# Attention block and two gated MLPs on one core: piece stores to GpSimd's queue, sum stores to SyncE's, another order on ScalarE

## The chip, the cores and the metric

One core of one Trainium2 chip runs the whole program. The metric is the device time of one execution in microseconds (us). Engines are called PE (TensorE), VectorE (DVE), ScalarE (ACT), GpSimd (POOL) and SyncE (SP); the last one computes nothing and only issues transfers.

## The reference

```python
B, H, S, Ns, D = 8, 8, 512, 32, 64          # x: B,H,S,D   state: B,H,Ns,D

# attention between tokens and a small state, both ways
a     = softmax(scale * x @ state.T)         # tokens look at the state
xread = a @ state
a2    = softmax(scale * state @ x.T)         # the state looks at tokens
sread = a2 @ x
x = concat([xread, sread], axis=2) -> (B * 544, 512)

h = x @ w_in;  x = (h * sigmoid(1.702 * h)) @ w_out      # first MLP, 512 -> 2048 -> 512
h = x @ w_in2; x = (h * cos(h)) @ w_out2                 # second MLP
```

All of it is to be computed to float32 accuracy. The weights come as 64-bit floats.

## The kernel before

**Numbers as two halves.** Every float32 factor of a large product is held as a rounded high half and the rest as a low half (`split_g`, `split_state`), and a product is three matmuls: high by high, high by low, low by high. ScalarE rounds the high half, VectorE subtracts for the low half.

**Tiles and steps.** The 4096 token rows are eight tiles of 512, one for each batch entry; the 256 state rows form a ninth, the tail tile (t = 8). A tile has 16 steps, one for each 128 columns of the hidden layer (c = 0 to 15). The first MLP (m = 0) goes through tiles 0 to 6, the tail tile, then tile 7; the second MLP (m = 1) follows. In each step `hidden` (line 341) makes one 128-wide slice of the hidden layer in PSUM, and `second` (line 422) adds the slice of two steps before (`LAG` = 2) into four PSUM accumulators. In between ScalarE and VectorE apply the gate: `gate` (line 371 on) in the first MLP, `cosine` (line 390) in the second. The order of instructions on each engine is the order in which the program is written, and each engine's queue is first in, first out.

**Decoding weights.** A 64-bit weight is turned into a float32 on the chip, in units of 128 x 1024. `decode_begin` (line 107) gives two ScalarE conversions (lines 117 and 122) and two VectorE bit operations (lines 125 and 128, called `bits`, at the end of the step). `decode_end` (line 134), one step later, rounds the high half on ScalarE (line 141) and subtracts for the low half on VectorE (line 143). Tile 0 decodes a unit in each of steps 0 to 13; the second MLP's weights are decoded in the tail tile, in tile 7 and in the first tile of the second MLP, one unit every second or third step.

**Pieces of state times weight.** For tiles 1 to 7 the state is multiplied into the first weight matrix beforehand, so that a slice of the hidden layer needs six matmuls and not 24 (line 353 in place of line 360). `sw_piece` (line 162) makes one of 64 pieces: six half-wide matmuls into a PSUM bank of the pool `psa` (two banks, shared with the attention's products), the rounding on ScalarE (line 174), the subtraction on VectorE (line 175), and one store to DRAM for each of two tiles (line 178). Its staging tile is two deep (tag `g`). `load_sw` (line 182) fetches the pieces back. The list `sw_steps` (line 503) says at which steps pieces are made; the attention for the next tile (`parts`, line 487) is spread over the same steps and takes banks of the same pool in turn.

**Sums.** At the end of a tile, `store` (line 441) copies each of the four accumulators to SBUF (`o`, two buffers) and stores it to DRAM (`yd`). This happens at step 1 of the next tile, and the accumulators are needed again at step 2. In the first MLP the store was issued on ScalarE's queue (line 446), in the second on SyncE's (line 449).

**Queues.** SyncE issues nearly everything in program order: weights (`fetch_w`), the attention's inputs (`load_xT`, `load_xN`), the pieces' stores and loads. GpSimd does little; among it are the four low halves of the tail tile's input (`split_tail`, line 456, subtraction at line 463), at step 14 of tile 6.

Of the kernel before, what the change touches and what calls it, by code (L numbers as in the profile page):

```python
# [24 lines left out]
KF = DFF // P  # L25
# [16 lines left out]
def attention_two_mlps(  # L42
# [12 lines left out]
    nc = tc.nc  # L55
# [78 lines left out]
    def decode_end():  # L134

        if not begun:
            return lambda: None
        m, nm, j = begun.pop(0)
        u = wt[m, nm, j]
        w = wp.tile([P, 2, UNIT], F32R, name=f"w{nm}{m}_{j}", tag=f"w{nm}{j}")  # L140
        nc.scalar.activation(out=w[:, 0, :], in_=u, func=AF.Copy)
        wt[m, nm, j] = (w[:, 0, :], w[:, 1, :])
        return lambda: nc.vector.tensor_tensor(out=w[:, 1, :], in0=u, in1=w[:, 0, :].bitcast(F32), op=ALU.subtract)
# [18 lines left out]
    def sw_piece(p, f, k):  # L162

        ps = ps_a.tile([P, S], F32, name="psS", tag="psa")
        for e in range(2):
            wh, wl = wt[0, "i", 2 * f + e]
            sl = slice(k * 2 * P, (k + 1) * 2 * P)
            out_ = ps[:, e * 2 * P:(e + 1) * 2 * P]
            for i, (l, r) in enumerate(((rhi, wh), (rhi, wl), (rlo, wh))):
                nc.tensor.matmul(out_, l[:, k, :], r[:, sl], start=(e == 0 and i == 0), stop=(e == 1 and i == 2),  # L170
                                 skip_group_check=True)
        o = ep.tile([P, 4, 2, P], F32R, name="swo", tag="g")
        pv = ps.rearrange("p (c f) -> p c f", f=P)
        nc.scalar.activation(out=o[:, :, 0, :], in_=pv, func=AF.Copy)
        nc.vector.tensor_tensor(out=o[:, :, 1, :], in0=pv, in1=o[:, :, 0, :].bitcast(F32), op=ALU.subtract)  # L175
        r0 = (k % 2) * D
        for i, b in enumerate(PAIRS[p]):
            nc.sync.dma_start(
                out=sw_dram[b, f][r0:r0 + D, :, k // 2, :], in_=o[i * D:(i + 1) * D].bitcast(F32).rearrange("p c h f -> p c (h f)")
            )  # L180

# [189 lines left out]
    def gate(t, c, stores, unit):  # L371

        ph = ht.pop((0, t, c))
        t1 = ep.tile([P, sizes[t]], F32, name="t1", tag="t1")
        nc.scalar.activation(out=t1, in_=ph, func=AF.Tanh, scale=0.5 * GATE)  # L375
        low_w = decode_end()
        g = t1
        nc.vector.scalar_tensor_tensor(out=g, in0=t1, scalar=1.0, in1=ph, op0=ALU.add, op1=ALU.mult)  # L378
        for s in stores[:1]:
            s()  # L380
        low = split_g(0, t, c, g)
        low_w()
        act, bits = decode_begin(*unit) if unit else ((lambda: None),) * 2
        act()
        low()
        for s in stores[1:]:
            s()
        return bits

    def cosine(t, c, stores, before, unit, end):  # L390

        ph = ht[1, t, c]
        r = ep.tile([P, sizes[t]], F32, name="r", tag="t1")
        d = ep.tile([P, sizes[t]], F32, name="d", tag="g")
        nc.scalar.activation(out=r, in_=ph, func=AF.Copy, scale=1.0 / (2.0 * math.pi), bias=0.25)  # L395
        low_w = decode_end()
        low = times(*before) if before else None
        if end:
            low()
        nc.vector.tensor_scalar(out=r, in0=r, scalar1=MAGIC, scalar2=MAGIC, op0=ALU.add, op1=ALU.subtract)  # L400
        for s in stores[:-1]:
            s()
        act, bits = decode_begin(*unit) if unit else ((lambda: None),) * 2
        nc.vector.scalar_tensor_tensor(out=d, in0=r, scalar=-TWO_PI_HI, in1=ph, op0=ALU.mult, op1=ALU.add)
        nc.vector.scalar_tensor_tensor(out=r, in0=r, scalar=-TWO_PI_LO, in1=d, op0=ALU.mult, op1=ALU.add)
        nc.vector.tensor_scalar(out=r, in0=r, scalar1=R_MIN, scalar2=R_MAX, op0=ALU.max, op1=ALU.min)  # L406
        nc.scalar.activation(out=r, in_=r, func=AF.Sin, bias=half_pi)  # L407
        act()
        if low and not end:
            low()  # L410
        low_w()
        for s in stores[-1:]:
            s()
        ht[1, t, c] = (ph, r)
        return bits

    def times(t, c):
        ph, r = ht.pop((1, t, c))
        nc.vector.tensor_tensor(out=r, in0=r, in1=ph, op=ALU.mult)  # L419
        return split_g(1, t, c, r)  # L420
# [20 lines left out]
    def store(m, t, k):  # L441
        n = sizes[t]
        o = op.tile([P, n if m == 0 else DM], F32, name="o", tag="o")
        nc.scalar.activation(out=o, in_=yt[k], func=AF.Copy, scale=0.5 if m == 0 else 1.0)  # L444
        if m == 0:
            nc.scalar.dma_start(out=y_dram[t][:, k, :], in_=o)
        elif t < B:
            r0 = t * TOK + k * P
            nc.sync.dma_start(out=out[r0:r0 + P, :], in_=o)
        else:  # L450
            per = P // NS
            for i in range(per):
                r0 = (k * per + i) * TOK + S
                nc.sync.dma_start(out=out[r0:r0 + NS, :], in_=o[i * NS:(i + 1) * NS, :])
# [23 lines left out]
    def warm(n):  # L478
# [22 lines left out]
    todo = {}  # L501

    sw_steps = (
        ((0, 1), [(0, c) for c in (2, 3, 4, 5, 7, 9, 11, 13, 15)] + [(1, c) for c in range(1, 8)]),
        ((1, 8), [(1, c) for c in (9, 11, 12, 13, 14, 15)] + [(2, c) for c in (0, 2, 3, 4, 5, 6, 8, 9, 10, 11)]),
        ((3, 1), [(t, c) for t in (3, 4) for c in (3, 4, 5, 9, 10, 11, 13, 14)]),
        ((5, 1), [(t, c) for t in (5, 6) for c in (3, 4, 5, 9, 10, 11, 13, 14)]),
    )
    todo_sw = {step: (p, n // 4, n % 4) for p, (_, at_) in enumerate(sw_steps) for n, step in enumerate(at_)}
    todo_split = {step: p for p, (step, _) in enumerate(sw_steps)}  # L510
    scores_of = [1, 0, *range(2, B)]

# [26 lines left out]
    with tc.manual_schedule():  # L539
# [34 lines left out]
        low_w = decode_end()  # L574
# [18 lines left out]
        fetches.update({steps[steps.index((0, B - 1, 0)) + 2 * j + 3]: (1, "o", j) for j in range(KF // 2)})  # L593
        at2 = [(0, B, c) for c in (8, 11, 14)] + [(0, B - 1, c) for c in range(1, KF, 2)] + [(1, 0, c) for c in range(0, 10, 2)]
        units.update({at_: (1, nm, j) for at_, (nm, j) in zip(at2, ((nm, j) for nm in "io" for j in range(KF // 2)))})
        loads_next = {9: (0,), 10: (1,), 11: (2,), 12: (3, 4), 13: (5,), 14: (6,), 15: (7,)}
        for i, (m, t, c) in enumerate(steps):
            if m == 0 and c == 0 and t + 1 < B:
                new_x(("a", t + 1), S, range(2))
                plan(i, t)  # L600
            if i + 1 < len(steps):
                hidden(m, t, c)
            if i + 2 == len(steps):
                hidden(*steps[-1])
            stores = second(*steps[i - LAG]) if i >= LAG else []
            unit = units.get((m, t, c))
            if m == 0:
                bits = gate(t, c, stores, unit)
            else:
                bits = cosine(t, c, stores, steps[i - 1][1:] if steps[i - 1][0] == 1 else None, unit, i + 1 == len(steps))  # L610
            if (m, t, c) in fetches:
                fetch_w(*fetches[m, t, c])
            if m == 0 and (t, c) in todo_split:
                split_state()
            if m == 0 and (t, c - 3) in todo_split and todo_split[t, c - 3] + 1 < len(PAIRS):
                load_pair(todo_split[t, c - 3] + 1)
            for b, name in todo.pop(i, ()):
                run_piece(b, int(name[-1]), name[:-2])
            if m == 0 and (t, c) in todo_sw:
                sw_piece(*todo_sw[t, c])  # L620
            bits()
            if m == 0:
                if t == 0 and c in (7, 9, 11, 13):
                    load_sw(1, (c - 7) // 2)
                if t == 0 and c == KF - 1:
                    for j in range(4, 8):
                        load_sw(1, j)
                if t == 1 and 5 <= c < 13:
                    load_sw(t, c + 3)
                if 1 < t < B and c + 8 < KF:  # L630
                    load_sw(t, c + 8)
                if 0 < t < B - 1:
                    for j in loads_next.get(c, ()) if t == 1 else (c - 8,):
                        if j >= 0:
                            load_sw(t + 1, j)
            if m == 0 and t == B - 2 and c == KF - 2:
                split_tail()
            j = i // KF
            if j + 1 < len(order) and i + KF >= len(steps1):
                if c == 2:  # L640
                    load_y(order[j + 1])
                if c in (7, 9, 11, 13):
                    split_y(order[j + 1], (c - 7) // 2, nc.gpsimd if m else nc.vector)
# [47 lines left out]
```

## Time and profile before

| | |
|---|---|
| median of 3 executions | 1566.74 us (1563.5 to 1567.01) |
| the profiled execution | 1568.79 us, its span 1567.0 us |
| PE busy | 1481.3 us, 95% of the span |
| VectorE, ScalarE, GpSimd busy | 962.5, 646.5, 44.0 us |
| mean granted TensorE clock | 0.978 |
| moved by DMA | 140.58 MB, mean 90 GB/s |

The page shows busy time in slices of the span, the longest chain of work, and groups of instructions by line. Matmuls overlap one another, so a busy PE is not a PE at its peak; but a stretch in which PE is idle or its clock is below 1.00 is time lost when PE sets the pace. The first MLP with the attention takes the first 810 us or so, the second MLP the rest.

### The profile page before, as it was taken

What the parts mean: (1) busy time and instruction counts of PE and PEld (TensorE: products, weight loads), DVE (VectorE), ACT (ScalarE), POOL (GpSimd) and SP (SyncE); (2) the same over time, 40 slices, a digit from 0 to 9 for tenths busy, and PEclk for the clock granted to TensorE, in tenths of its full rate; (3) what the DMA queues carried; (4) which work ended last, traced back from release to release, by engine and by line L of the source; (5) the groups of instructions that cost most, each with busy time, mean ns of one, the idle gap of its engine ahead of it and who ended that gap; (6) DMA issues with size and microseconds to landing.
All of it is one profiled execution on the core that took longest, in us unless ns stands there. A gap on an engine that the chain in (4) does not pass through costs nothing.

```text
span 1567.0 us, 19260 instructions
## 1 busy us (share of the span) xinstructions
PE 1481.3 (95%) x7306; PEld 1204.5 (77%) x7306; DVE 962.5 (61%) x1674; ACT 646.5 (41%) x1078; POOL 44.0 (3%) x43
## 2 busy tenths in 40 slices
PE   7988988999999999997989999999999999999998
PEld 5766767777777777786767788888888888888886
DVE  6876454545555464525678766666667666666665
ACT  4664333333433333334665433334344333343433
POOL 0000000000000000000000101000001010000000
PEclk8989999999999999999999999999999999999999
DMA  9654556554555444354430010101010101010000
GB/s 302 186 161 121 145 151 180 153 141 138 141 158 135 123 107 121 84 177 146 168 134 1 1 55 1 54 1 41 0 43 13 41 1 55 0 54 1 27 1 27
DMA packets 102844, 140.58 MB, mean 90 GB/s; under 512 B 11616, under 2 KB 67040, under 8 KB 102752
## 3 DMA queue, kind: packets, MB, share of 16 engines
q1 hardware_dynamic: 97280, 130.05, 28.9%
q10 hardware_dynamic: 5472, 9.31, 1.6%
q8 instruction: 57, 0.93, 0.3%
q14 instruction: 35, 0.29, 0.1%
HBM read 92.14 MB, written 47.19 MB: 89 GB/s over the span
## 4 chain that ended last, share of the span: by engine, by line
PE 68%; DVE 15%; ACT 7%; DMA 5%; issue 3%; SPq 0%; ACTq 0%; DVEq 0%
PE py L438 35%; PE ph L360 23%; PE ph L353 7%; DMA yd<-o 3%; PE psS L170 2%; ACT gh L367 2%; DVE gl L369 2%; DVE u L125 2%; DVE u L128 2%; ACT o L444 1%; DVE swo L175 1%; DVE t L378 1%; PE psC L313 1%; ACT u L117 1%; ACT rawo L122 1%
## 5 line engine op out<-in xcount | busy, mean ns | idle before, releaser
L360 PE MATMUL ph<-xh,wi 128*128 128x512 f32 (+1 forms) x1280 | 407.9, 382 | 0.2 <-DVE t L378 0.2
L438 PE MATMUL py<-gh,wo 128*128 128x512 f32 (+1 forms) x1152 | 372.3, 385 | 27.1 <-ACT o L444 19.3
L438 PE MATMUL py<-wo,gh 128*128 128x512 f32 x1088 | 337.8, 392 | 4.8 <-ACT o L444 4.5
L360 PEld LDWEIGHTS ph<-xh,wi 128*128 128x128 f32 x1280 | 240.1, 190 | 50.4 <-issue 1.9
L438 PEld LDWEIGHTS py<-gh,wo 128*128 128x128 f32 x1152 | 217.7, 192 | 75.6 <-ACT o L444 23.1
L360 PE MATMUL ph<-xl,wi 128*128 128x512 f32 (+1 forms) x640 | 243.2, 382 | 0.0
L438 PEld LDWEIGHTS py<-wo,gh 128*128 128x128 f32 x1088 | 203.4, 189 | 48.9 <-ACT o L444 7.3
L438 PE MATMUL py<-gl,wo 128*128 128x512 f32 (+1 forms) x576 | 221.6, 385 | 1.8 <-DVE gl L369 1.8
L438 PE MATMUL py<-wo,gl 128*128 128x512 f32 x544 | 213.8, 393 | 5.0 <-DVE gl L369 4.9
L407 ACT ACTIVATE r<-r,half_pi 128x512 f32<-128x512 f32 (+1 forms) x144 | 100.9, 701 | 241.7 <-DVE r L406 241.3
L369 DVE TENSOR_TENSOR gl<-t,gh 128x512 fp32r<-128x512 f32 (+1 forms) x144 | 95.3, 662 | 162.6 <-ACT gh L367 162.6
L367 ACT ACTIVATE gh<-t 128x512 fp32r<-128x512 f32 (+1 forms) x144 | 87.2, 606 | 238.7 <-PE py L438 137.5
L400 DVE TENSOR_SCALAR r<-r 128x512 f32<-128x512 f32 (+1 forms) x144 | 64.0, 444 | 178.2 <-ACT r L395 177.9
L353 PE MATMUL ph<-xh,swt 128*128 128x512 f32 x448 | 163.5, 406 | 2.9 <-DMA swt<-sd 2.5
L395 ACT ACTIVATE r<-ph 128x512 f32<-128x512 f32 (+1 forms) x144 | 82.4, 572 | 169.9 <-PE ph L360 169.3
L378 DVE SCALAR_TENSOR_TENSOR t<-t,ph 128x512 f32<-128x512 f32 (+1 forms) x144 | 93.9, 652 | 89.7 <-ACT t L375 89.5
L360 PEld LDWEIGHTS ph<-xl,wi 128*128 128x128 f32 x640 | 121.9, 191 | 23.2
L438 PEld LDWEIGHTS py<-gl,wo 128*128 128x128 f32 x576 | 110.6, 192 | 23.9 <-DVE gl L369 3.5
L438 PEld LDWEIGHTS py<-wo,gl 128*128 128x128 f32 x544 | 102.5, 188 | 30.7 <-DVE gl L369 9.8
L419 DVE TENSOR_TENSOR r<-r,ph 128x512 f32<-128x512 f32 (+1 forms) x144 | 94.7, 658 | 44.9 <-ACT r L407 44.8
L375 ACT ACTIVATE t<-ph 128x512 f32<-128x512 f32 (+1 forms) x144 | 82.0, 570 | 86.9 <-PE ph L353 67.1
L353 PEld LDWEIGHTS ph<-xh,swt 128*128 128x128 f32 x448 | 86.7, 194 | 31.4 <-issue 6.9
(77 smaller groups left out, 1471.7 us busy)
## 6 DMA issues: line engine op xcount, KB each, us to landing
sd<-swo SPq DMA_DIRECT2D x112, 256.0 KB, 3.3
swt<-sd SPq DMA_DIRECT2D x112, 256.0 KB, 4.6
rawi<-in_w_in SPq DMA_DIRECT2D x32, 512.0 KB, 5.4
rawo<-in_w_out SPq DMA_DIRECT2D x32, 512.0 KB, 4.6
xT_t<-in_xT SPq DMA_DIRECT2D x36, 256.0 KB, 4.3
xN_t<-in_xN SPq DMA_DIRECT2D x16, 512.0 KB, 3.9
yd<-o ACTq DMA_DIRECT2D x32, 256.0 KB, 3.4
yraw<-yd SPq DMA_DIRECT2D x32, 256.0 KB, 4.4
```

Of the source, the lines that this page charges most:

```text
L125: nc.vector.scalar_tensor_tensor(out=ui, in0=ui, scalar=3, in1=low, op0=ALU.logical_shift_left, op1=ALU.bitwise_or)
L353: nc.tensor.matmul(ph, l, r, start=(g == 0 and i == 0), stop=(g == 1 and i == 2))
L360: nc.tensor.matmul(ph, w[:, f0:f0 + P], x, start=(w is wh and k == 0 and x is xk[0][0]), stop=(w is wl and k == KD - 1))
L367: nc.scalar.activation(out=gh, in_=g, func=AF.Copy)
L369: return lambda: nc.vector.tensor_tensor(out=gl, in0=g, in1=gh.bitcast(F32), op=ALU.subtract)
L375: nc.scalar.activation(out=t1, in_=ph, func=AF.Tanh, scale=0.5 * GATE)
L378: nc.vector.scalar_tensor_tensor(out=g, in0=t1, scalar=1.0, in1=ph, op0=ALU.add, op1=ALU.mult)
L395: nc.scalar.activation(out=r, in_=ph, func=AF.Copy, scale=1.0 / (2.0 * math.pi), bias=0.25)
L400: nc.vector.tensor_scalar(out=r, in0=r, scalar1=MAGIC, scalar2=MAGIC, op0=ALU.add, op1=ALU.subtract)
L407: nc.scalar.activation(out=r, in_=r, func=AF.Sin, bias=half_pi)
L419: nc.vector.tensor_tensor(out=r, in0=r, in1=ph, op=ALU.mult)
L438: nc.tensor.matmul(yt[k], l, r, start=(c == 0 and i == 0), stop=(c == KF - 1 and i == 2))
```

## The change

It has four parts. The stores of the pieces are issued on GpSimd's queue in place of SyncE's. The stores of the first MLP's sums are issued on SyncE's queue in place of ScalarE's. In `gate` and `cosine` the gate's own work (`split_g`, `times`) comes ahead of `decode_end` on ScalarE, and in `gate` the low half of a weight (`low_w`) comes after the gate's low half on VectorE. The 64 pieces are made at other steps, sometimes two in one step, and with them the steps at which the state is split and the pieces of tile 1 and 2 are fetched.

```diff
         for i, b in enumerate(PAIRS[p]):
-            nc.sync.dma_start(
+            nc.gpsimd.dma_start(
                 out=sw_dram[b, f][r0:r0 + D, :, k // 2, :], in_=...
             )
...  gate
         nc.scalar.activation(out=t1, in_=ph, func=AF.Tanh, scale=0.5 * GATE)
-        low_w = decode_end()
         g = t1
         nc.vector.scalar_tensor_tensor(out=g, in0=t1, scalar=1.0, in1=ph, op0=ALU.add, op1=ALU.mult)
         for s in stores[:1]:
             s()
         low = split_g(0, t, c, g)
-        low_w()
+        low_w = decode_end()
         act, bits = decode_begin(*unit) if unit else ((lambda: None),) * 2
         act()
         low()
+        low_w()
         for s in stores[1:]:
             s()
...  cosine
+        low = times(*before) if before else None
         low_w = decode_end()
-        low = times(*before) if before else None
...  store
         if m == 0:
-            nc.scalar.dma_start(out=y_dram[t][:, k, :], in_=o)
+            nc.sync.dma_start(out=y_dram[t][:, k, :], in_=o)
...  sw_steps
-        ((0, 1), [(0, c) for c in (2, 3, 4, 5, 7, 9, 11, 13, 15)] + [(1, c) for c in range(1, 8)]),
-        ((1, 8), [(1, c) for c in (9, 11, 12, 13, 14, 15)] + [(2, c) for c in (0, 2, 3, 4, 5, 6, 8, 9, 10, 11)]),
-        ((3, 1), [(t, c) for t in (3, 4) for c in (3, 4, 5, 9, 10, 11, 13, 14)]),
-        ((5, 1), [(t, c) for t in (5, 6) for c in (3, 4, 5, 9, 10, 11, 13, 14)]),
+        ((0, 1), [(0, c) for c in (2, 4, 6, 7, 7, 10, 11, 11, 13, 13, 15)] + [(1, c) for c in (2, 3, 6, 8, 9)]),
+        ((1, 10), [(1, c) for c in range(12, KF)] + [(2, c) for c in (2, 4, 5, 6, 9, 10, 11, 12, 14, 15)] + [(3, 0), (3, 2)]),
+        ((3, 3), [(3, c) for c in (6, 9, 10, 12, 14, 15)] + [(4, c) for c in (2, 4, 6, 9, 10, 12, 14, 15)] + [(5, 0), (5, 2)]),
+        ((5, 4), [(5, c) for c in (6, 9, 10, 12, 14, 15)] + [(6, c) for c in (2, 4, 5, 6, 9, 10, 11, 12, 14, 15)]),
...  main loop
-        loads_next = {9: (0,), 10: (1,), 11: (2,), 12: (3, 4), 13: (5,), 14: (6,), 15: (7,)}
+        loads_next = {10: (0,), 11: (1,), 12: (2,), 13: (3, 4), 14: (5,), 15: (6, 7)}
...
-                if t == 0 and c in (7, 9, 11, 13):
-                    load_sw(1, (c - 7) // 2)
+                if t == 0 and c in (9, 11, 13, 14):
+                    load_sw(1, (c - 8) // 2)
...
-                if t == 1 and 5 <= c < 13:
+                if t == 1 and 5 <= c < 9:
                     load_sw(t, c + 3)
+                if t == 1 and 10 <= c < 14:
+                    load_sw(t, c + 2)
```

## Rows read from the trace of the kernel before

**Rows 1.** Busy time by stretch: tiles 1, 2, 3, tail, 7 (stretch, its length, engines, clock).
```profile
142.00:258.00 116.00, 102.29 (x583) 79.71 (x582) 58.36 (x130) 40.02 (x72) 0.00 (x0) 0.93 0.57 159
258.40:342.00 83.60, 77.44 (x414) 62.08 (x413) 42.08 (x83) 29.25 (x52) 0.00 (x0) 0.96 0.57 155
342.00:424.50 82.50, 77.46 (x426) 62.34 (x425) 43.28 (x85) 30.45 (x55) 0.00 (x0) 1.00 0.51 139
670.00:727.50 57.50, 52.61 (x397) 50.44 (x396) 23.94 (x42) 24.26 (x47) 0.00 (x0) 0.97 0.55 173
727.50:808.00 80.50, 73.25 (x302) 57.65 (x301) 53.28 (x63) 47.21 (x65) 0.00 (x0) 0.96 0.40 132
```

**Rows 2.** Waits, whole span: who waited for whom, us, times, longest.
```profile
PE py L438 <- ACT o L444: 23.8, 11, 4.6
...
SPq L178 <- DVE swo L175: 349.0, 62, 14.1
```

**Rows 3.** Timeline of VectorE and ScalarE, tile 0, steps 7 to 9 (start, duration).
```profile
78.01 1.22 DVE L128 SCALAR_TENSOR_TENSOR u<-rawo,u 128x1024 int32<-128x1024 int32 x1
79.15 0.68 DVE L378 SCALAR_TENSOR_TENSOR t<-t,ph 128x512 f32<-128x512 f32 x1
...
79.33 1.06 ACT L141 ACTIVATE wo<-u 128x1024 fp32r<-128x1024 f32 x1 [2.73 <-DVE u L128]
80.29 0.61 ACT L367 ACTIVATE gh<-t 128x512 fp32r<-128x512 f32 x1
80.81 1.12 ACT L117 ACTIVATE u<-rawi 128x1024 f32<-128x1024 f32 x1
...
86.66 1.06 ACT L141 ACTIVATE wi<-u 128x1024 fp32r<-128x1024 f32 x1 [2.73 <-DVE u L128]
...
92.91 1.06 ACT L141 ACTIVATE wo<-u 128x1024 fp32r<-128x1024 f32 x1 [1.63 <-DVE u L128]
```

**Rows 4.** PE's timeline and chain: pieces that waited, one that did not.
```profile
97.68 0.76 PE L170 MATMUL psS<-wi,rhi 128*128 128x256 f32 x2 [4.31 <-DVE xs L324]
...
141.29 0.71 PE psS L170 x6
...
400.71 0.50 PE L170 MATMUL psS<-wi,rhi 128*128 128x256 f32 x2 [1.74 <-DVE swo L175]
```

**Rows 5.** Timeline of SyncE's queue and of PE, start of tile 1.
```profile
145.14 1.17 SPq L178 DMA_DIRECT2D sd<-swo  x2
...
149.28 0.86 SPq L214 DMA_DIRECT2D xT_t<-in_xT  x2
...
155.53 2.69 PE L229 MATMUL psA<-xT_t,sblk 128*32 128x512 f32 x8 [4.11 <-DMA xT_t<-in_xT]
```

**Rows 6.** Timeline of the sum stores at step 1 of tile 3.
```profile
347.59 0.33 ACTq L446 DMA_DIRECT2D yd<-o  x1
...
348.29 1.06 SPq L187 DMA_DIRECT2D swt<-sd  x2
...
352.37 0.60 ACT L444 ACTIVATE o<-py 128x512 f32<-128x512 f32 x1 [3.82 <-DMA yd<-o]
...
353.02 0.50 PE L438 MATMUL py<-gh,wo 128*128 128x512 f32 x1 [1.99 <-ACT o L444]
```

**Rows 7.** Transfers by line: count, KB each, median us to landing.
```profile
sd<-swo SPq DMA_DIRECT2D x112, 256.0 KB, 3.3
...
yd<-o ACTq DMA_DIRECT2D x32, 256.0 KB, 3.4
...
out<-o SPq DMA_DIRECT2D x32, 256.0 KB, 2.0
```

**Rows 8.** Timeline of GpSimd, VectorE and PE, end of tile 6.
```profile
662.74 2.83 POOL L463 TENSOR_TENSOR xtail<-xs,xtail 128x256 fp32r<-128x256 f32 x4 [650.90 <-ACT xtail L462]
...
664.16 0.69 DVE L175 TENSOR_TENSOR swo<-psS,swo 128x512 fp32r<-128x512 f32 x1
...
665.67 1.59 PE L360 MATMUL ph<-xtail,wi 128*128 128x256 f32 x12
```

More of the change, by code (lines that the diff above doesn't have):

```diff
@@ L503, in attention_two_mlps @@
     sw_steps = (
-        ((0, 1), [(0, c) for c in (2, 3, 4, 5, 7, 9, 11, 13, 15)] + [(1, c) for c in range(1, 8)]),
-        ((1, 8), [(1, c) for c in (9, 11, 12, 13, 14, 15)] + [(2, c) for c in (0, 2, 3, 4, 5, 6, 8, 9, 10, 11)]),
-        ((3, 1), [(t, c) for t in (3, 4) for c in (3, 4, 5, 9, 10, 11, 13, 14)]),
-        ((5, 1), [(t, c) for t in (5, 6) for c in (3, 4, 5, 9, 10, 11, 13, 14)]),
-    )
-    todo_sw = {step: (p, n // 4, n % 4) for p, (_, at_) in enumerate(sw_steps) for n, step in enumerate(at_)}
+        ((0, 1), [(0, c) for c in (2, 4, 6, 7, 7, 10, 11, 11, 13, 13, 15)] + [(1, c) for c in (2, 3, 6, 8, 9)]),
+        ((1, 10), [(1, c) for c in range(12, KF)] + [(2, c) for c in (2, 4, 5, 6, 9, 10, 11, 12, 14, 15)] + [(3, 0), (3, 2)]),
+        ((3, 3), [(3, c) for c in (6, 9, 10, 12, 14, 15)] + [(4, c) for c in (2, 4, 6, 9, 10, 12, 14, 15)] + [(5, 0), (5, 2)]),
+        ((5, 4), [(5, c) for c in (6, 9, 10, 12, 14, 15)] + [(6, c) for c in (2, 4, 5, 6, 9, 10, 11, 12, 14, 15)]),
+    )
+    todo_sw = {}
+    for p, (_, at_) in enumerate(sw_steps):
+        for n, step in enumerate(at_):
+            todo_sw.setdefault(step, []).append((p, n // 4, n % 4))
     todo_split = {step: p for p, (step, _) in enumerate(sw_steps)}
@@ L618, in attention_two_mlps @@
                 run_piece(b, int(name[-1]), name[:-2])
-            if m == 0 and (t, c) in todo_sw:
-                sw_piece(*todo_sw[t, c])
+            for piece in todo_sw.get((t, c), ()) if m == 0 else ():
+                sw_piece(*piece)
             bits()
             if m == 0:
-                if t == 0 and c in (7, 9, 11, 13):
-                    load_sw(1, (c - 7) // 2)
+                if t == 0 and c in (9, 11, 13, 14):
+                    load_sw(1, (c - 8) // 2)
                 if t == 0 and c == KF - 1:
```

## The prediction

> **What bounds the kernel now.** I read the busy time by stretch first, one stretch per token tile. The second MLP, from about 880 us on, has PE busy without a gap and is left alone. So the question is what the first MLP loses. In the tiles of [rows 1] PE idles 13.7 us of 116.0 in tile 1 (stretch less busy time), 6.2 in tile 2, 5.0 in tile 3 (tiles 4 to 6 are built alike), 4.9 in the tail tile and 7.3 in tile 7; where it has idled long, the granted clock falls to its lower level too (mean 0.93 in tile 1, 1.00 in tile 3). With the clock counted as lost time, (1 - 0.93) x 116 = 8.1 us more in tile 1, 3.3 in tile 2, 1.7 in the tail tile, 3.2 in tile 7. Then I read who ends PE's waits. Three causes come back: sums whose copy to SBUF is late [rows 2], pieces of state times weight whose PSUM bank is not yet empty [rows 4], and loads that are late because SyncE's queue stood at the store of a piece, 349 us in all [rows 2, 5]. Tile 0 is different: there PE waits for the decoded weights, and the bound is a loop between ScalarE and VectorE [rows 3].
>
> **ScalarE's order, tile 0.** Per step the loop is: VectorE ends the bits of one unit (78.01 + 1.22 = 79.23), ScalarE rounds it (79.33), copies the gate (80.29), starts the next unit (80.81), VectorE combines that. After the change the gate's copy comes first, and it needs VectorE's product, which stands behind the same bits and ends at 79.15 + 0.68 = 79.83. The copy then starts at about 79.9 and holds ScalarE 0.52 (80.29 to 80.81), so the rounding starts at 80.4 instead of 79.3, and the next unit 0.96 later (79.33 to 80.29) at 81.4 instead of 80.8: **+0.6 us a step** [rows 3]. The gate's low half gains about 1 us in VectorE's order, but in tile 0 PE does not wait for it. Thirteen links of this loop lie one behind another: 13 x 0.55 = +7 us (0.55, since some links go through VectorE, where about 0.5 is added). Ends: 0 if PE's waits swallow it, +14 if the weights' low half, now last on VectorE, doubles it. With 7.3 us for a step with a piece and 6.3 for the next without [rows 3], a piece costs the loop about 1.0; tile 0 has two more of them, +2. Against that the piece of step 9 goes, with its stall of 4.3 us [rows 4], some 3 us on the loop. Tile 0: **+6 us**. In the tail tile and in tile 7, where a unit comes every second or third step and PE keeps the pace, the earlier low half removes short waits, about 2 us, counted below. In the second MLP the swap changes no order on VectorE: 0.
>
> **Pieces at other steps.** The banks of the two-deep pool rotate. In tiles 3 to 5 a piece at step 5 or 11 took the bank of the piece one step earlier, whose second half VectorE reads last in a crowded step; the wait at 400.71 is one of six, 1.74 us [rows 4]. The new lists leave out step 5 and 11 there, and nearly all banks are two steps old. In tiles 2 and 6, with ten pieces each, steps 5 and 11 are still used, so about 2 us stay. Tile 1 has four pieces fewer, 4 x 0.71 = -2.8 [rows 4].
>
> **Pieces stored from GpSimd.** SyncE no longer stands at VectorE's result. In tile 1 the store of the last piece of tile 0 went out at 145.14, four weight loads followed, and the x load at 149.28, for which PE then stood 4.1 us [rows 5], and ran at the lower clock behind. Without the store those four loads go earlier, and the x load waits only for PE's own scores. The cost of a store on GpSimd is not in this trace. Below: -0.6, its own queue saves the second issue behind the first (0.6 of the 1.17 for two). Above: a whole VectorE step, 7.3 us [rows 3], if GpSimd gets through only when VectorE pauses. I take 1 to 2 us over the 3.3 us of today [rows 7], nearest to GpSimd's own short operations (2.83 / 4 = 0.7 each, [rows 8]). What hides it: a piece is read back four or more steps later, except the one at step 9 of tile 1, fetched at step 10 and used at 12, where I count some 2 us to spare. If that cover goes, each us is lost once; the staging buffers are two deep, so ScalarE would wait too once a store takes over 8 us.
> Queued behind such a store on GpSimd are the four low halves of the tail's input. They started at 662.74 and took 2.83; the tail's first matmul came at 665.67 [rows 8]. Now they stand behind the store of a piece at the same step, whose VectorE half ends about 664.9, and so end near 669: **+2 us**, a new wait.
>
> **Sums stored from SyncE.** The third and fourth sum copies reuse two buffers and wait for the first two stores. In tile 3 the second store was issued at 347.59 on ScalarE's queue while x and weight loads were issued on SyncE's (348.29), landed about 352.3, and ScalarE stood 3.82, PE 1.99 [rows 6]. After the change the four stores stand in SyncE's queue ahead of those loads, which are not needed for several steps. A store of the same size from SyncE lands in 2.0 us at the median in the quieter second MLP, against 3.4 here [rows 7]. With 2.5, the fourth copy comes about 2 us earlier and most of PE's wait is gone. What SyncE now waits for (the fourth copy) delays x and weight loads by some 3 us, hidden by six steps.
> By the Trainium skill, "DMA: Bandwidth & Descriptors", section "Issuing engines are not separate DMA queues", DMAs from several engines interleave on the same 16 DMA engines, and another issuer saves only issue time. That speaks against a gain from the new queue as such; the gain above comes from the order in one queue, and the rule's own outcome is the third rival.
>
> **The sum.** Tile 0 +6. Tile 1: 13.7 idle, 8.1 clock, 2.8 pieces = 24.6, of which I take 21. Tile 2: 6.2 + 3.3 = 9.5, less 2 that stay: -7. Tiles 3 to 5: 3 x 5.0 = 15, take -13. Tile 6: its stores -1, the two added pieces +1.4: 0. Tail tile: 4.9 + 1.7 = 6.6, take -5, and +2 for GpSimd: -3. Tile 7: 7.3 + 3.2 = 10.5, of which one 2 us wait stays and a part of the clock with it: -6. Total 6 - 21 - 7 - 13 - 3 - 6 = **-44 us**. The profiled execution took 1568.8 us, 2.1 above the median of the three runs; 1566.7 - 44 = **1523 us**.
>
> **Rivals.** (1) GpSimd as the bound, slower than before: with two staging buffers, 64 pieces need 32 store times in a row. The first MLP's pieces span about 630 us, so the loss starts at 630 / 32 = 20 us a store; at 22 it is 32 x 22 = 704, some 75 us more than now: 1640. For it: each piece is two transfers of 1 KB rows; against: a POOL operation of 0.7 us and 3.3 us for the whole store today. 0.04.
> (2) Stores from GpSimd held up by VectorE: late by most of a step, 7 us. Then the piece of step 9 in tile 1 stalls PE by some 5 us, the tail's low halves by 5 more, and double pieces in tile 0 make ScalarE wait: 12 us given back, 1535. 0.13.
> The Trainium skill, "SBUF — State Buffer", section "Who interferes with whom", tells of this: descriptors that GpSimd writes are starved while VectorE holds the shared ports in a 2-port mode. It also says that an operation with two tensor inputs does not hold the write side, and most of VectorE's work here is of that form, hence the small chance.
> (3) The stores' landing does not get shorter, since what slows it is the traffic and not the order: of the -44, 18 came from stores (4 in tile 2, 5 in tiles 3 to 5, 4 in the tail, 5 in tile 7): 1541. 0.13.
> (4) ScalarE's order costs double in tile 0 (+14): 1531. 0.08.
> (5) The change is nearly empty, since another chain takes over in tiles 1 to 5; against it stands that ScalarE is busy 40 of 116 us there and VectorE 58 [rows 1]. 1563 to 1570. 0.03.
>
> **How the numbers follow.** The forecast has 0.59. Its own range is 1512 to 1533: the end below takes all idle and clock time of tiles 1 to 7. With rivals 2 to 4 the range is **1508 to 1545**. A measurement of this kernel tells about 0.3% from no change, 4.7 us. Faster: 0.59 + 0.13 + 0.13 + 0.08 = 0.93, less a little for mixtures, 0.92. Same 0.03. Slower 0.05, nearly all rival 1.
>
> **What would show it.** Right: the bank waits of the pieces nearly gone from PE's waits, PE's wait on sum copies down from 23.8 us [rows 2] to under 10, no wait for the x load at the start of tile 1, mean clock of tile 1 near 0.98; tile 0 some 6 us longer, with ScalarE's wait for VectorE now ahead of the gate's copy. Wrong: landings of the pieces over 8 us, ScalarE waiting for a staging buffer, or landings of the sums still over 4 us.

## The result and the profile after

The changed kernel takes 1528.4 us at the median (1525.9 to 1530.3), the kernel before 1566.9: a ratio of 0.9755, with a 95% interval of 0.9729 to 0.9781, so 38.5 us less where 44 were forecast. The profiled execution took 1530.3 us, with a span of 1528.5.

The table gives each tile's length, taken from the first tanh of a tile to the first tanh of the next in ScalarE's timeline (for MLP2's first tile from its first copy of the hidden sum). The last column is a kernel of the first experiment: the changed one with ScalarE's old order.

| us | before | after | difference | forecast | old order |
|---|---|---|---|---|---|
| tile 0 | 118.2 | 123.8 | +5.6 | +6 | 115.1 |
| tile 1 | 107.7 | 88.6 | -19.1 | -21 | 88.8 |
| tile 2 | 88.5 | 80.9 | -7.6 | -7 | 81.0 |
| tiles 3 to 5 | 246.6 | 231.3 | -15.3 | -13 | 231.1 |
| tile 6 | 81.0 | 81.9 | +0.9 | 0 | 81.9 |
| tail tile | 57.3 | 55.4 | -1.9 | -3 | 54.2 |
| tile 7 | 77.4 | 77.7 | +0.3 | -6 | 70.4 |
| first tile of MLP2 | 97.5 | 95.7 | -1.8 | 0 | 95.2 |

Busy time of the changed kernel in tiles 1, 2, 3, the tail and 7 (stretch, length, busy time of PE, weight loads, VectorE, ScalarE and GpSimd, then the granted clock and the DMA columns), to be held against [rows 1]. The stretches of [rows 1] are limited otherwise (its tile 1 is 116.0 us long, 107.7 by the tanh); by the limits of the table PE idled 13.7, 6.2, 5.0, 4.2 and 7.9 us in these five tiles of the kernel before:

```profile
149.50:238.20 88.70, 85.34 (x520) 66.79 (x519) 50.15 (x110) 33.72 (x63) 10.73 (x18) 0.98 0.58 167
238.20:319.10 80.90, 78.60 (x438) 63.74 (x437) 45.74 (x94) 31.21 (x56) 11.95 (x20) 1.00 0.59 165
319.10:396.30 77.20, 77.01 (x426) 62.19 (x425) 43.32 (x85) 30.56 (x55) 9.56 (x16) 1.00 0.57 156
632.30:687.70 55.40, 52.05 (x396) 49.88 (x395) 23.12 (x41) 23.23 (x46) 0.59 (x1) 1.00 0.57 181
687.70:765.40 77.70, 69.56 (x293) 55.44 (x292) 50.17 (x58) 44.09 (x65) 0.00 (x0) 0.96 0.42 139
```

In tile 3 PE idles 0.2 us where it idled 5.0, and tile 1's clock went from 0.93 to 0.98. Tile 7 still idles 8.1 us, the most of the five, with the clock at 0.96. The waits over the whole span (who waited for whom, us in total, times, longest) name what is left:

```profile
POOL sd L178 <- DVE swo L175: 545.5, 61, 35.8
...
PE py L438 <- ACT o L444: 9.8, 5, 5.3
PE py L438 <- ACT wo L141: 9.6, 6, 3.2
...
PE psS L170 <- DVE swo L175: 7.1, 6, 1.7
...
PE ph L353 <- DVE t L377: 5.1, 5, 1.5
```

The wait on sum copies fell from 23.8 us [rows 2] to 9.8. SyncE's 349.0 us at piece stores have become GpSimd's 545.5, for which PE waits 0.4 us in all (twice, for the tail's low halves). The pieces' wait for `xs` [rows 4] is gone. PE's wait for `t` has grown: five times and 5.1 us in this row, twice and 2.2 us at line 360, all in the tail tile and tile 7, where it was three times 0.2 us. Transfers by line (queue, count, KB, median us to landing) show that sums land earlier (3.4 before) and pieces 0.5 us later (3.3 before) [rows 7]:

```profile
sd<-swo POOLq DMA_DIRECT2D x112, 256.0 KB, 3.8
...
yd<-o SPq DMA_DIRECT2D x32, 256.0 KB, 2.6
```

And the x load at the start of tile 1 no longer holds PE: 0.22 us in this timeline (start, duration) where it was 4.11 [rows 5].

```profile
153.17 0.82 SPq L214 DMA_DIRECT2D xT_t<-in_xT  x2
...
157.68 1.60 PE L229 MATMUL psA<-xT_t,sblk 128*32 128x512 f32 x8 [0.22 <-DMA xT_t<-in_xT]
```

### The profile page after: what moved, and what is told of

It is laid out like the page before. It is cut to its first block, busy times and chain, and to the rows that moved or that the text cites. A ratio compares the mean times of both kernels' runs of the same rounds, so it can differ in the third digit from the quotient of the medians.

```text
span 1528.5 us, 19319 instructions
## 1 busy us (share of the span) xinstructions
PE 1466.0 (96%) x7306; PEld 1195.1 (78%) x7306; DVE 966.3 (63%) x1674; ACT 644.1 (42%) x1078; POOL 110.8 (7%) x155
## 4 chain that ended last, share of the span: by engine, by line
PE 74%; DVE 13%; ACT 7%; DMA 3%; issue 3%; SPq 0%; POOL 0%; ACTq 0%; DVEq 0%
PE py L438 38%; PE ph L360 23%; PE ph L353 8%; PE psS L170 2%; DVE u L125 2%; DVE u L128 2%; DVE t L377 1%; DMA yd<-o 1%; ACT u L117 1%; ACT gh L367 1%; PE psC L313 1%; ACT rawo L122 1%; PE psA L229 1%; DVE gl L369 1%; DVE wo L143 1%
## 5 line engine op out<-in xcount | busy, mean ns | idle before, releaser
L438 PE MATMUL py<-gh,wo 128*128 128x512 f32 (+1 forms) x1152 | 368.2, 382 | 17.0 <-ACT wo L141 9.6
L438 PEld LDWEIGHTS py<-gh,wo 128*128 128x128 f32 x1152 | 214.8, 190 | 65.6 <-ACT wo L141 12.1
L367 ACT ACTIVATE gh<-t 128x512 fp32r<-128x512 f32 (+1 forms) x144 | 87.6, 608 | 300.8 <-DVE t L377 185.9
L369 DVE TENSOR_TENSOR gl<-t,gh 128x512 fp32r<-128x512 f32 (+1 forms) x144 | 97.5, 677 | 166.7 <-ACT gh L367 166.7
L377 DVE SCALAR_TENSOR_TENSOR t<-t,ph 128x512 f32<-128x512 f32 (+1 forms) x144 | 93.9, 652 | 84.3 <-ACT t L375 84.2
L438 PEld LDWEIGHTS py<-wo,gl 128*128 128x128 f32 x544 | 102.5, 188 | 30.5 <-DVE gl L369 9.4
L375 ACT ACTIVATE t<-ph 128x512 f32<-128x512 f32 (+1 forms) x144 | 82.0, 569 | 83.3 <-PE ph L353 69.8
```

What stands on the lines that cost most here:

```text
L367: nc.scalar.activation(out=gh, in_=g, func=AF.Copy)
L369: return lambda: nc.vector.tensor_tensor(out=gl, in0=g, in1=gh.bitcast(F32), op=ALU.subtract)
L438: nc.tensor.matmul(yt[k], l, r, start=(c == 0 and i == 0), stop=(c == KF - 1 and i == 2))
```

## The experiments

Two questions were open: why tile 7 gained nothing, and whether each of the four parts does what the prediction says. Each part was done alone on the kernel before and undone from the whole. The changed kernel with the old ScalarE order turned out to be the fastest, and it serves as the base of the later runs.

**ScalarE's old order, the rest as changed.**

```diff
+        low_w = decode_end()
         g = t1
         nc.vector.scalar_tensor_tensor(out=g, ...)
...
         low = split_g(0, t, c, g)
-        low_w = decode_end()
+        low_w()
         act, bits = ...
         act()
         low()
-        low_w()
```

(and the same two calls turned back in the cosine.)

> The changed kernel with the ScalarE order of the kernel before put back in both functions (the weight's high half ahead of the gate's). Theory: the new order costs time in two places, about 6 us in tile 0 (118.2 us before, 123.8 after) and about 6 us in tile 7, where VectorE's low half of the weight now comes last and holds up the next gate product and the PSUM bank that it frees (five PE waits of 0.8 to 1.5 us for that product after, 0.2 us before); it gives back some 2 us in the tail tile. Undoing it should give 1517 to 1520 us, tile 0 at 118 to 119 us, tile 7 at 71 to 73 us, and PE's waits for the gate product t at 0.2 us each. Rival: the order is neutral; tile 0 is longer because of its two more pieces and tile 7 is unchanged because its sum stores no longer matter there. Then 1527 to 1530 us, tiles 0 and 7 as after (124 and 78 us).

Measured: 1511.6 us (1511.5 to 1512.1), ratio to the kernel before 0.9643 (0.9628 to 0.9657), below the 1517 to 1520 expected. It beats the changed kernel by 16.8 us and is the version to keep. Tile 7 falls to 70.4 us, the tail to 54.2 and tile 0 to 115.1, below the 118 to 119 expected: the order costs 8.7 us there and 7.3 in tile 7. The rival falls. The mechanism shows in one unit's timeline in tile 7, first of the changed kernel (tanh is L375, the gate's product `t` L377, or L378 with the old order, the gate's high and low half L367 and L369, the weight's L141 and L143):

```profile
738.52 0.68 DVE L377 SCALAR_TENSOR_TENSOR t<-t,ph 128x512 f32<-128x512 f32 x1
...
739.25 0.50 PE L353 MATMUL ph<-xh,swt 128*128 128x512 f32 x1 [1.50 <-DVE t L377]
...
739.29 0.63 ACT L367 ACTIVATE gh<-t 128x512 fp32r<-128x512 f32 x1 [2.81 <-DVE t L377]
...
739.83 1.04 ACT L141 ACTIVATE wi<-u 128x1024 fp32r<-128x1024 f32 x1
...
739.96 0.69 DVE L369 TENSOR_TENSOR gl<-t,gh 128x512 fp32r<-128x512 f32 x1 [0.76 <-ACT gh L367]
...
740.91 1.23 DVE L143 TENSOR_TENSOR wi<-u,wi 128x1024 fp32r<-128x1024 f32 x1 [0.26 <-ACT wi L141]
742.05 0.68 DVE L377 SCALAR_TENSOR_TENSOR t<-t,ph 128x512 f32<-128x512 f32 x1
...
748.52 0.68 DVE L377 SCALAR_TENSOR_TENSOR t<-t,ph 128x512 f32<-128x512 f32 x1
```

and then with the old order:

```profile
732.84 1.06 ACT L141 ACTIVATE wo<-u 128x1024 fp32r<-128x1024 f32 x1 [1.60 <-DVE u L128]
...
733.27 0.68 DVE L378 SCALAR_TENSOR_TENSOR t<-t,ph 128x512 f32<-128x512 f32 x1
...
733.94 1.23 DVE L143 TENSOR_TENSOR wo<-u,wo 128x1024 fp32r<-128x1024 f32 x1
...
734.00 0.50 PE L353 MATMUL ph<-xh,swt 128*128 128x512 f32 x1 [0.20 <-DVE t L378]
...
734.04 0.63 ACT L367 ACTIVATE gh<-t 128x512 fp32r<-128x512 f32 x1
...
735.68 0.68 DVE L378 SCALAR_TENSOR_TENSOR t<-t,ph 128x512 f32<-128x512 f32 x1
```

With the old order ScalarE rounds the weight while VectorE makes the product, and VectorE takes the weight's low half while ScalarE copies the gate, so VectorE is not idle between a unit's first product (733.27) and its second (735.68): 2.41 us. With the new one ScalarE stands 2.81 us for the product, VectorE 0.76 for the copy and 0.26 for the rounding, and the low half (1.23) ends just ahead of the second product: 3.53 us (738.52 to 742.05). From the second product to the next unit's first it is 6.5 us with either order (742.05 to 748.52; 726.79 to 733.27 with the old one). So the loop of the two engines is 1.1 us longer a unit, and PE, which needs the PSUM bank that the first product frees, starts 10.00 us apart (739.25, 749.25) against 8.89 with the old order (725.11, 734.00). With the old order, as in the kernel before, PE waits 0.2 us there, so the loop was already as long as PE's work.

**The new order alone, on the kernel before** (the mirror of the diff above).

> The kernel before with the new ScalarE order alone. Theory: tile 0 longer by some 7 us (13 steps of 0.55 us), tile 7 by some 5 us, the tail tile shorter by 2 us: 1574 to 1578 us. Rival (the order is neutral, and the losses of tiles 0 and 7 come from the pieces and the queues): 1565 to 1569 us.

Measured: 1582.3 us, ratio 1.0092 (1.0075 to 1.0109): 15 us slower, more than expected. Tile 0 takes 127.1 us (+8.9), tile 7 82.2 (+4.8), the tail 58.1 (+0.8, where 2 us less was expected). In tile 7 the same three waits for `t`, of 1.5 to 1.6 us, stand in PE's timeline.

**The weight's low half on GpSimd in the tail and tile 7, new order.**

```diff
-        low_w = decode_end()
+        low_w = decode_end(nc.gpsimd if t >= B - 1 else nc.vector)
...
```

(and `decode_end` makes the low half on the engine that it is given.)

> The changed kernel (1528.4 us), with the low half of the decoded weight computed on GpSimd in place of VectorE in the gates of the tail tile and tile 7 (those units are MLP2's, needed much later). Theory: in tile 7 VectorE's low half, which under the new order waits for ScalarE's later high half, holds up the next gate product t and its PSUM bank; with it off VectorE's queue, PE's four or five waits of 0.8 to 1.5 us for t in tile 7 fall to 0.2 us or none, tile 7 goes from 77.7 to 70 to 73 us: 1521 to 1524 us. Rival: t is late because ScalarE itself is late (its queue order), then the waits stay and the time is 1527 to 1530 us.

Measured: 1523.9 us (1523.7 to 1524.5). Tile 7 goes to 73.2 us, so 4.5 of the 7.3 us come back, in the range that was expected. But the waits for `t` do not fall to 0.2 us: three of 0.94 to 0.98 stay, 9.43 us apart (735.54, 744.97). VectorE's low half is thus about half of the 1.1 us a unit. The other half stays with the order on ScalarE, as the rival has it: with nothing ahead of it on VectorE, the second product now waits for its tanh, which stands behind the weight's rounding:

```profile
737.68 0.69 DVE L377 SCALAR_TENSOR_TENSOR t<-t,ph 128x512 f32<-128x512 f32 x1 [0.74 <-ACT t L375]
```

The gate's low half took 1.07 us beside GpSimd's work here, and 0.69 elsewhere; the next run shows why.

**The same with the old order.** (the same diff on the fast version)

> The kernel with the old ScalarE order (1511.6 us), with the same low halves on GpSimd. Theory: VectorE's queue is then free of 1.2 us per unit, the three waits for gl in the tail tile (0.54, 0.60, 0.65 us) and the three for t in tile 7 (0.2 us each) go: 1508 to 1511 us. Rival: GpSimd and VectorE side by side slow each other, or MLP2's first steps wait for the low halves: 1512 to 1516 us.

Measured: 1526.8 us, 15.2 slower than the version it was made from; a miss. Tile 7 takes 81.8 us. Timeline of one unit:

```profile
716.09 2.37 POOL L143 TENSOR_TENSOR wi<-u,wi 128x1024 fp32r<-128x1024 f32 x1 [7.73 <-ACT wi L141]
...
716.56 2.45 DVE L369 TENSOR_TENSOR gl<-t,gh 128x512 fp32r<-128x512 f32 x1 [1.11 <-ACT gh L367]
718.93 0.68 DVE L378 SCALAR_TENSOR_TENSOR t<-t,ph 128x512 f32<-128x512 f32 x1
...
719.06 0.50 PE L438 MATMUL py<-gl,wo 128*128 128x512 f32 x1 [1.63 <-DVE gl L369]
```

GpSimd's subtraction runs from 716.09 to 718.46. VectorE's subtraction of half the size, started within it, ends 0.55 us behind it and takes 2.45 us in place of 0.69. The rival's first half (the two slow each other) holds for VectorE; that GpSimd is slowed too is not shown.

**Sums from SyncE alone, on the kernel before.**

```diff
-            nc.scalar.dma_start(out=y_dram[t][:, k, :], in_=o)
+            nc.sync.dma_start(out=y_dram[t][:, k, :], in_=o)
```

> The kernel before with the MLP sums stored from SyncE alone (pieces still on SyncE at their old steps). Theory: the store leaves ScalarE's queue and lands earlier, so PE waits less for the o buffers, but SyncE still stands at the piece stores for 349 us in all, and a sum's store queued behind one comes later; 10 to 16 us less: 1551 to 1557 us, tiles 3 and 5 shorter by 4 to 5 us each, tiles 1, 2 and 4 by less. Rival (the landing is the transfer's own time and the queue changes nothing): 1565 to 1569 us.

Measured: 1548.5 us, ratio 0.9876 (0.9859 to 0.9892), 18.6 less, beyond the expected 10 to 16. The stores land in 2.6 us. Tiles 3 to 5 gain 2.7 to 2.9 each, less than expected, and tile 7 gains 7.0, to 70.4; tiles 1 and 2 gain nothing. In these two the first two stores stand on SyncE behind stores and loads of pieces, and at the start of tile 1 they land no earlier than from ScalarE (transfers issued from 151 to 156 us):

```profile
xT_t<-in_xT SPq DMA_DIRECT2D x2, 256.0 KB, 6.3
yd<-o SPq DMA_DIRECT2D x2, 256.0 KB, 5.9
```

**Sums back on ScalarE's queue, from the fast version.** (the same line turned back)

> The old ScalarE order, new steps, pieces from GpSimd, but MLP1's sums stored from ScalarE's queue as before. Theory: the store's landing goes back from 2.6 to 3.4 us, the staging buffers come free later and PE waits for the sum copies at every tile's start: 14 to 19 us more than 1511.6 (18.4 us were gained by the sums alone): 1526 to 1531 us, tiles 3 to 5 at 79 to 80 us and tile 7 at 77 us. Rival: with SyncE free of the pieces the sums' queue matters less: 1516 to 1522 us.

Measured: 1536.7 us (1532.5 to 1538.5), 25.1 more, beyond the expected 14 to 19. Tiles 3 to 5 take 78.9 to 80.7 us and tile 7 75.7. PE's waits and the landing of the sums:

```profile
PE py L438 <- ACT o L444: 21.6, 14, 4.5
```

```profile
yd<-o ACTq DMA_DIRECT2D x32, 256.0 KB, 3.6
```

With 2.6 us the same wait is 8.3 in all, so 13.3 us of the loss stand in this wait; the rest was not followed row by row. The move of the sums to SyncE is worth 19 to 25 us of the whole.

**Pieces stored from GpSimd alone, on the kernel before.**

```diff
-            nc.sync.dma_start(
+            nc.gpsimd.dma_start(
                 out=sw_dram[b, f][r0:r0 + D, :, k // 2, :], in_=...
```

> The kernel before with the pieces stored from GpSimd alone. Theory: SyncE no longer stands at piece stores, so the x load at tile 1's start is early (its 4.1 us wait of PE goes, and the half-clock stretch behind it), and nothing else changes: 5 to 9 us less, 1558 to 1562 us, tile 1 at 99 to 103 us, the other tiles as before; a piece's stores land in 4 to 6 us. Rivals: GpSimd's stores stand behind VectorE's work and land late, PE waits for pieces: 1570 us and more; or the x load's wait has another cause and nothing changes: 1565 to 1569 us.

Measured: 1565.2 us over ten runs, ratio 0.9991 (0.9981 to 1.0001), which cannot be told from no change. Tile 1 gains the 6.6 us expected (101.1) and the x load's wait is gone, but a piece now waits right there for its bank, for as long as the two together did before (4.11 for the x load and 1.05 for the piece):

```profile
156.69 0.80 PE L170 MATMUL psS<-wi,rhi 128*128 128x256 f32 x2 [5.21 <-ACT a L293]
```

So the gain of tile 1 does not come from the x load: two waits for loads of pieces (1.51 and 0.95 us before) are gone, and the tile's mean clock is 0.97 where it was 0.92. Tiles 2 to 4 and 6 are longer by 0.3 to 1.8 us each. In tiles 3 and 4 the mean clock is 0.98 in place of 1.00; in tile 6 PE waits 1.05 us for the tail's low halves, which now stand behind a piece's store.

**Pieces back on SyncE, from the fast version.** (the same line turned back)

> The old ScalarE order, sums from SyncE, new steps, but pieces stored from SyncE as before. Theory: SyncE again stands at each piece's store until VectorE's low half is done, and the x loads and the loads of pieces queue behind it: PE waits for the x load at tile 1's start (0.2 us without, 4 us with) and a half-clock stretch follows; 5 to 10 us more than 1511.6: 1517 to 1522 us. Rival: at the new steps the stores come early enough, GpSimd's queue is worth nothing (as it was worth 1.9 us alone): 1510 to 1514 us.

Measured: 1528.4 us, 16.8 more, beyond the expectation. Tile 1 takes 102.1 us where it took 88.8, which is 13.2 of the loss. PE's waits show more than the x load:

```profile
PE ph L353 <- DMA swt<-sd: 8.2, 3, 5.2
...
PE psA L229 <- DMA xT_t<-in_xT: 3.9, 1, 3.9
```

At the new steps the loads of pieces for tile 1 are issued later, and behind SyncE's stands they come too late: one wait is of 5.21 us, and the clock is lower behind these waits (tile 1's mean is 0.93 here, 0.98 in the fast version).

**The new steps alone, on the kernel before** (the lists of steps of the diff, with nothing else).

> The kernel before with the new steps of pieces and loads alone (pieces stored from SyncE, sums from ScalarE, old order). From the parts left out one by one (the steps are worth 25.4 us beside the two other gains, GpSimd 16.8 us there but 1.9 us alone) the steps and GpSimd need each other: alone the steps should give 25.4 - (16.8 - 1.9) = about 10 us: 1553 to 1560 us, with PE's wait for xs ahead of pieces gone but waits for loads of pieces in tile 1 in its place. Rival: the steps give their whole worth alone: 1540 to 1545 us.

Measured: 1546.3 us, ratio 0.9872 (0.9858 to 0.9887): 21.0 less, twice what was expected; the rival's 1540 to 1545 was nearer. Tile 0 is at 115.1, tile 1 at 102.5, tile 2 at 82.6, tiles 3 to 5 at 78.8 to 81.1. The same 5.21 us wait for a load stands in tile 1.

**The old steps, from the fast version** (the lists turned back).

> The old ScalarE order, sums from SyncE, pieces from GpSimd, but pieces and loads at the old steps. By the sum of the parts alone (sums -18.4 us, GpSimd -1.9 us) it should be 1545 to 1549 us, tile 1 at 100 to 102 us and tile 2 at 88 to 89 us, with PE's 12 us of waits for xs ahead of pieces back; the new steps are then worth 34 to 37 us, most of it in tiles 1 and 2. Rival: the steps are worth little by themselves and GpSimd's queue together with the sums on SyncE does the work: 1515 to 1525 us.

Measured: 1537.0 us, 25.4 more. Tile 1 takes 99.8, tile 2 84.0; PE's wait of pieces for `xs` is back with 12.1 us. The rival falls, and so does the sum of parts made there, 1545 to 1549: sums and GpSimd give 30 us together, 20.5 one by one.

**Each GpSimd store in four, from the fast version.**

```diff
-            nc.gpsimd.dma_start(out=sw_dram[b, f][r0:r0 + D, :, k // 2, :], in_=o[i * D:(i + 1) * D] ...)
+            for c in range(4):
+                nc.gpsimd.dma_start(out=sw_dram[b, f][r0:r0 + D, c:c + 1, k // 2, :], in_=o[i * D:(i + 1) * D, c:c + 1] ...)
```

> The kernel with the old ScalarE order (1511.6 us), with each GpSimd store of a piece split into four stores of a quarter each: GpSimd's issue per piece goes from 1.2 us to some 4.8 us, with the same bytes. The prediction's margins: all pieces have far more than 4 us to spare except the one at step (1,9), whose load is already late by 2.7 us (PE's wait ahead of step (1,12)); each further us should be lost there once, with what the half clock behind it adds: 3.6 to 6 us more, 1514 to 1518 us, and no other tile longer by over 1 us but tile 7's start (the tail's low halves on GpSimd). Rival: GpSimd becomes the bound, pieces queue up on it and loads are late in tiles 1 to 6 as well: 1520 us and more.

Measured: 1517.9 us (1515.2 to 1521.3), 6.3 more. The time fits the expectation, its place does not. GpSimd, SyncE and PE around step (1,12):

```profile
190.70 8.23 POOL L179 DMA_DIRECT2D sd<-swo  x16 [5.47 <-DVE swo L175]
...
196.24 0.38 SPq L221 DMA_DIRECT2D xN_t<-in_xN  x1
...
198.48 4.01 SPq L189 DMA_DIRECT2D swt<-sd  x6
...
204.37 0.47 PE L355 MATMUL ph<-xh,swt 128*128 128x512 f32 x1 [3.01 <-DMA swt<-sd]
```

The two pieces end 4.6 us later on GpSimd than with whole stores (194.29), and PE's wait is 3.01 us against 2.70. What makes the load late is SyncE, which stands 21.5 us for the buffer of `xN` until 196.2, then issues three loads first. In the profiled execution (3.6 us more) the rest is the tail's low halves on GpSimd, for which PE waits 1.39 us more (tile 6 +1.6), and 0.7 in tile 7.

**Two small edits to the fast version.**

```diff
-   ... [(1, c) for c in (2, 3, 6, 8, 9)]
+   ... [(1, c) for c in (2, 3, 6, 8, 8)]
...
+        if m == 0 and k % 2:
+            nc.vector.tensor_scalar(out=o, in0=yt[k], scalar1=0.5, scalar2=None, op0=ALU.mult)
+        else:
             nc.scalar.activation(out=o, in_=yt[k], ...)
```

> The kernel with the old ScalarE order (1511.6 us) and two small edits: the last piece of the first pair at step (1,8) instead of (1,9), and two of the four sum copies at the end of a tile on VectorE instead of ScalarE. Theory: the load of (1,12) is issued no later than SyncE is free, PE's 2.7 us wait there shrinks to 0 to 1.5 us and the half-clock stretch behind it may go; the copies no longer queue behind the decode on ScalarE where the tail tile, tile 7 and MLP2 begin (PE waits 1.5, 2.0 + 0.6 and 3.7 us): 1503 to 1509 us. Rival: VectorE's queue takes the place of ScalarE's and the two pieces at one step wait for each other's bank: 1510 to 1515 us.

Measured: 1520.2 us (1518.4 to 1520.5), 8.6 more: the rival holds, by more than it said. Tile 1 is longer by 5.7 us and the tail by 2.5. In tile 1 the second piece at step 8 waits 2.47 us for its bank, the tile's mean clock falls from 0.98 to 0.96, and the load of (1,12) is still 2.42 us late. For the sum copies PE now waits on both engines:

```profile
PE py L438 <- DVE o L445: 5.7, 8, 2.2
...
PE py L438 <- ACT o L447: 4.3, 3, 3.7
```

## Why the prediction was right, and where it was not

The parts, in us (minus is faster; alone: against the kernel before; in the whole: the fast version against the same without that part, and for ScalarE's order the changed kernel against the fast version):

| part | alone | in the whole |
|---|---|---|
| sums from SyncE | -18.6 | -25.1 |
| new steps | -21.0 | -25.4 |
| pieces from GpSimd | -1.9 | -16.8 |
| ScalarE's order | +15.2 | +16.8 |

**ScalarE's order, tile 0.** The loop of [rows 3] was read rightly and undersized: 8.7 to 8.9 us against +7. In the other direction the pieces of tile 0 gave 3.1 us (118.2 to 115.1) where +2 - 3 = -1 was counted, so the tile's sum, +6 against +5.6, came out by two errors that cancel. Rival 4, the double cost, did not come. PE's side of it is the 9.6 us for `wo` in the waits above (2.9 with the old order).

**ScalarE's order, tail and tile 7.** This is the step that failed. The text says that a unit comes there only every second or third step, that PE keeps the pace, and that the earlier low half of the gate removes short waits of about 2 us. The waits for `gl` in the tail do go (0.54, 0.60 and 0.65 us with the old order), but waits for `t` of 0.73 and 1.07 come in their place. In tile 7 PE did not keep the pace by any margin: the loop of ScalarE and VectorE took 8.89 us a unit and PE already waited 0.2 for it, so the 1.1 us that the order adds to the loop count in full. The order costs 7.3 us there: 4.9 in PE's waits for `t` (5.5 against 0.6), the rest with the stretch at the lower clock (mean 0.96 against 1.00) behind a 2.60 us wait for a sum copy. With the old order PE waits as long there in two parts (2.01 and 0.64) and the clock stays up; why is not shown. Without the order tile 7 gains 7.0 us from the stores, where 6 were counted for the tile. The prediction looked at which low half PE waits for and not at what stands behind the last one on VectorE: the next product, and with it the loop. Tile 7 is 6.3 us off in the sum, which is off by 5.5 in all; the other tiles' errors nearly cancel.

**Pieces at other steps.** Right: the wait for `xs` is gone; six waits of up to 1.74 us for `swo` stay, the longest of them in tiles 2 and 6, as told. "Nearly gone" was too much for the pieces as a whole: their waits on banks went from 26.3 to 11.3 us, and 6.6 of these now stand in tile 0, where two pieces share a step. Tiles 3 to 5 gained 15.3 (13 taken): their idle time went to nearly nothing.

**Pieces from GpSimd.** The x load's wait went, as told, and the store costs what was taken or less: 0.5 us more until landing, 0.61 us of GpSimd for each of the 112 stores. But the text has the whole value in that one load. It is 1.9 us alone, where a piece waits in the x load's place, and 16.8 with the new steps, which make the loads of pieces late unless SyncE is free. The two parts need each other, and the prediction counted them apart; its tile 1 (-21, measured -19.1) holds because it took nearly all of the idle and clock time. Of its covers, the one at (1,9) did fail as feared, 2.41 us in the changed kernel, but not by GpSimd's doing, as the split stores show: SyncE is busy with `xN`. The +2 for the tail's low halves was too much. They start right behind the store, and PE waits 0.17 and 0.18 us:

```profile
628.13 0.58 POOL L178 DMA_DIRECT2D sd<-swo  x1 [11.26 <-DVE swo L175]
628.72 2.80 POOL L463 TENSOR_TENSOR xtail<-xs,xtail 128x256 fp32r<-128x256 f32 x4
...
630.21 1.19 PE L360 MATMUL ph<-xtail,wi 128*128 128x256 f32 x6 [0.17 <-POOL xtail L463]
```

PE reads the four halves one after another, each soon after GpSimd has made it, where the prediction let it wait for the last.

**Sums from SyncE.** Right in the mechanism and the total: 2.6 us measured, 2.5 taken, and 18 us of gain forecast against 18.6 alone. The places were not right, so the close total is in part luck: alone tile 2 gains nothing (4 forecast), tiles 3 to 5 gain 8.3 (5), the tail 3.1 (4), tile 7 7.0 (5). Rival 3 falls, since the landing did get shorter: the same 256 KB land in 3.3 to 3.6 us from ScalarE's queue in five kernels and in 2.6 or 2.7 from SyncE's in nine, with the pieces on either queue. That it is the order, and not ScalarE's queue as such, shows in single stores of the kernel before, first one that was issued alone at the start of tile 4 (427 to 429 us), then the next two (430 to 431.8), beside loads from SyncE:

```profile
yd<-o ACTq DMA_DIRECT2D x1, 256.0 KB, 2.3
...
xT_t<-in_xT SPq DMA_DIRECT2D x2, 256.0 KB, 3.9
yd<-o ACTq DMA_DIRECT2D x2, 256.0 KB, 5.2
swt<-sd SPq DMA_DIRECT2D x2, 256.0 KB, 5.8
```

Over the fourteen kernels, a 256 KB store of the sums of tiles 0 to 6 with no other transfer issued from 3 us before it to 2 us after lands in 2.5 us at the median from ScalarE's queue (55 stores) and in 2.4 from SyncE's (126); with others in that time it takes 4.7 and 3.2. In SyncE's queue the loads stand behind the copy that SyncE waits for, and so come later. The trace agrees here with the rule of the Trainium skill ("DMA: Bandwidth & Descriptors", section "Issuing engines are not separate DMA queues") that another issuer saves only issue time: the queue as such changed nothing in the landing, the order did. What ScalarE gains by no longer issuing (0.33 us a store [rows 6]) was not told apart.

**Rivals 1, 2 and 5.** GpSimd with four times the issues cost 6.3 us and is far from a bound. Its stores were not held up by VectorE: they landed in 3.8 us. The change was not empty, since tiles 1 to 5 gained 42.0 us. MLP2's first tile, put at 0 in the sum, gained 1.8, which the sums' stores account for: with these back on ScalarE's queue it takes 97.5 us again.

## What to carry to other kernels

Ahead of swapping two operations on an engine, list for each of its partners in the loop what comes last in its queue afterwards, and who waits for the thing behind that; here the operation put last stood ahead of the next product, in a loop that was already as long as PE's work. Two edits that feed one queue (loads that may come later, and a queue that no longer stands) are to be priced together: one by one they gave 1.9 and 21.0 us, and the first was worth 16.8 beside the second. An engine with 545 us of waits costs nothing as long as nobody waits for it, and where a store's buffer is needed again at once, loads that are not needed yet belong behind it: beside such loads a store landed in 4.7 us and alone in 2.5, from the same queue.

## What the hardware showed that was not expected

A VectorE subtraction with both inputs in SBUF, 128x512, took 2.45 us beside a GpSimd subtraction of 128x1024 (2.37 us) and 0.69 us elsewhere, while the product that reads one input from PSUM kept its 0.69 us beside the same subtraction (changed kernel with the low halves on GpSimd, 737.68). The trace agrees here with the Trainium skill, "SBUF — State Buffer", section "Who interferes with whom", by which an operation of VectorE with two SBUF inputs contends with a GpSimd instruction that reads SBUF. GpSimd's stores cost VectorE nothing that shows: with 91 of them in tiles 1 to 6, 95 of the 96 gate subtractions of the fast version take 0.693 us at the mean, as all 96 do before; the one left ran beside the tail's low halves and took 2.66. Splitting a store in four cost GpSimd 0.51 us for each part (8.23 us for 16) against 0.61 for a whole one.
